# One more row's sums on ScalarE, one more front pair in plain form, and new hand-written orders

## The chip, the core and the metric

The program runs on one core of a Trainium2 chip. A core has a matrix engine (TensorE, PE in the profile; its weight loads are PEld), VectorE (DVE), ScalarE (ACT), GpSimd (POOL) and SyncE (SP), which here only issues DMAs. Each engine works through its own list of instructions in order and waits for the others by semaphores. Matmul results go to PSUM, which has eight banks of 512 float32 per partition; all else is kept in SBUF. The metric is the time of the program on the device in microseconds, lower is better. The kernel before takes 345.87 us, the median of three runs from 345.47 to 346.12.

## What is computed

Four residual blocks on one tensor of 2048 rows and 512 columns: a spectral filter A, a mixer B, then both again with the same weights. "Layer" below means one A and one B.

```python
def _A_ref(x, w_r, w_i):
    B, S, D = x.shape
    X = (lambda x, axes=(-2,-1): jnp.fft.rfft2(x.astype(jnp.float32), axes=axes))(x, axes=(-2, -1))
    W = w_r + 1j * w_i
    X = X * W
    y = (lambda x, s, axes=(-2,-1): jnp.fft.irfft2(x, s=s, axes=axes).astype(jnp.bfloat16))(X, (S, D), axes=(-2, -1))
    return y

def _B_ref(x, w1, w2, w3, w4):
    ...
    h = _gelu(_layernorm(x, axis=-1) @ w1)
    ...
    hs = jnp.concatenate([g0, g1, g2, g3], axis=-1) @ w2
    x1 = x + hs
    h2 = _gelu(_layernorm(x1, axis=-1) @ w3) @ w4
    return x1 + h2

x = A_x
x = x + _A_ref(_layernorm(x, axis=-1), A_w_r, A_w_i)
x = x + _B_ref(_layernorm(x, axis=-1), B_w1, B_w2, B_w3, B_w4)
x = x + _A_ref(_layernorm(x, axis=-1), A_w_r, A_w_i)
x = x + _B_ref(_layernorm(x, axis=-1), B_w1, B_w2, B_w3, B_w4)
```

`g0` to `g3` are quarters of the columns of `h`, shifted by one or two rows down or up. The FFTs are done as matmuls with tables of cosines and sines.

## The kernel before

Row s of x is held as s = 16 p + q: partition p, and one of 16 "rows" q of 128 x 512 elements. In the mixers row n of the order `ROWS` is q = n + 2 modulo 16. The kernel schedules nothing by itself: three strings, ORDER_0, ORDER_A and ORDER_B, list the steps, and each step appends its instructions to the engines concerned. So a step's place in the string is its place in the list of every engine that it uses. A step is a letter, a number, for some an engine (A ScalarE, V or D VectorE, P GpSimd), and after a point the PSUM bank.

- ORDER_0, the first front. `s` takes the sums of a row: by bn_stats on VectorE, or for rows in `ON_ACT` by two passes of ScalarE (lines 353 and 290), of which `f` makes mean and variance on GpSimd (lines 359 to 361). `i` aggregates (line 306), `S` is the square root on ScalarE, `J` the reciprocal on VectorE (line 368). These work by groups of rows, `GROUPS`. `Q` multiplies the DFT table by a row's 1/std into one of eight buffers Tq (lines 384, 386), `O` is the front's matmuls of a pair of rows (line 403), `G` and `L` copy the result to V (lines 152, 154; `L` is the second half of a split copy).
- ORDER_A and ORDER_B, layers 1 and 2. A: `d` (lines 544 to 550) and its copy `t`, `q` (line 568) and its copy `x`, the product with the filter `p` (line 587 from the copy; line 584 straight from PSUM when its engine is D), `b` and `V` (line 598) with copies `m` and `l`; then `D` and `C` (line 618), the copy `Y`, `P` (line 646), and `a` (line 654), which adds to x and takes the sums. B: `s` squares on ScalarE, `r`, `e`, `i`, `M`, `c` make 1/std, `n` normalises, `T` is the transposing DMA on SP (line 674), which is how rows turn into columns; `v` (line 686) multiplies by w1, `h` is gelu; `u` (line 702) multiplies by w2, `f` adds, `k` squares, `R`, `o`, `U` are the second norm and its transposing DMAs, `w` (line 737) multiplies by w3, `g` is gelu, `W` (line 757) multiplies by w4, `A` (line 763) adds to x. At the end of layer 2 `y` stores; at the end of layer 1 come the statistics `B`, `j`, `S`, `J` and the front of layer 2 (`Q`, `O`, `G`, `L`). `X` is so many matmuls on zeros.
- `over_p_quarters` and `over_p_plain` are two forms of the front. The quarters form folds inside the matmuls: a row takes four matmuls of 256 columns and four of 128, and ScalarE or VectorE copies to V. The plain form takes four matmuls of 128 columns a row; the right half is copied by ScalarE (`G..A`), two subtractions and an addition follow on VectorE (`G..V`, lines 424, 425), and `I` folds again (line 435). `PLAIN` says how many pairs of layer 2's front have it: pairs 0 to 5 of 0 to 6; rows 14 and 15 stand alone. A pair in `SPLIT_V` is copied in halves.

Transposing DMAs and stores share SP's list. V's buffer is that of xn. The copies t, X's junk rows, Y, `right` and `pairs` share four buffers of one tag (TV_Y).

Of the kernel before, what the change touches and what calls it, by code (L numbers as in the profile page):

```python
# [11 lines left out]
ACT = mybir.ActivationFunctionType  # L12
ALU = mybir.AluOpType
BF16 = dt.bfloat16
FP32 = dt.float32

P = 128
# [358 lines left out]
            self.K.nc.scalar.activation(dst, src, ACT.Identity, bias=self.mr[:, i, :], scale=r)  # L376

def scaled_T(K, q, r, eng="V"):

    K.Tq[q] = K.stream.tile([P, 2, P], BF16, name="Tq", bufs=8)
    if eng in "VP":
        e = K.nc.vector if eng == "V" else K.nc.gpsimd
        e.tensor_scalar(K.Tq[q][:], K.T[:], r, None, op0=ALU.mult)
    else:
        K.nc.scalar.activation(K.Tq[q][:], K.T[:], ACT.Copy, bias=0.0, scale=r)  # L386

def over_p_quarters(K, qs):

    n = len(qs)
    ps = banks(K, 2)
    for i, q in enumerate(qs):
        T = K.Tq.pop(q)
        plus, both, swap = [v.rearrange("d k (b c) -> d k b c", c=4) for v in (T[:], T[:], T[:, ::-1])]
        plus = plus[:, 0]
        twice = lambda k: T[:, k:k + 1].to_broadcast([P, 2, P]).rearrange("d k (b c) -> d k b c", c=4)
        for h in range(2):
            o = ps[:, h, 0:256 * n].rearrange("d (k b q c) -> d k b q c", k=2, q=n, c=4)[:, :, :, i]
            terms = ((0, o, twice(0)), (1, o[:, 1], plus), (3, o[:, 1], plus), (2, o, swap)) if h == 0 else \  # L400
                    ((1, o, swap), (0, o[:, 0], plus), (2, o[:, 0], plus), (3, o, twice(1)))
            for j, (c, dst, rhs) in enumerate(terms):
                K.nc.tensor.matmul(dst, lhsT=K.x[:, q, c * P:(c + 1) * P], rhs=rhs, start=(j == 0), stop=(j == 3))  # L403
    return ps[:, :, 0:256 * n]

def over_p_plain(K, qs):

    ps = banks(K, len(qs))
    for i, q in enumerate(qs):  # L410
# [41 lines left out]
def first_front(K):  # L452
# [71 lines left out]
def layer(K, last):  # L524
# [4 lines left out]
    V = K.V  # L529
# [6 lines left out]
    tv, X, pab, Y, xT, xT3, gT, ln, ln3, lnA = [{} for _ in range(10)]  # L536
# [251 lines left out]

    def scale_T(n, eng):
        k, i = divmod(n, 4) if n < 12 else (n, 0)  # L790
        scaled_T(K, ROWS[n], lnA[k].r[:, i:i + 1], eng)

    def front(k):
        qs = [ROWS[n] for n in PAIRS[k]]
        ps["O", k] = over_p_plain(K, qs) if k < PLAIN else over_p_quarters(K, qs)

    def take_front(k, eng, half=0):
        if "V" not in next_V:
            next_V["V"] = new_V(K)
        qs = [ROWS[n] for n in PAIRS[k]]  # L800
        if k < PLAIN:
            if eng == "A":
# [40 lines left out]
WAKE = 30  # L843
FILL = {}
GROUPS = [[0, 1], [2, 3], [4, 5, 6, 7], [8, 9, 10, 11], [12, 13], [14, 15]]
ON_ACT = [5, 9]
TABLES = 2
FIRST = [[0, 1], [2, 3], [4, 5], [6, 7], [8, 9], [10, 11], [12, 13], [14], [15]]
UNITS = {b: [b, b + 1] if 2 <= b < 14 else [b] for b in (0, 1, 2, 4, 6, 8, 10, 12, 14, 15)}
# [3 lines left out]
LATE = ((14, 15), (0, 14))  # L853
SPLIT_B = ((12, 13, 14, 15), (12, 13, 14, 15))
SPLIT_FIRST = (5, 6, 7, 8)
SPLIT_V = (6, 14, 15)
ROWS = [*range(2, 16), 0, 1]
PAIRS = {**{k: [2 * k, 2 * k + 1] for k in range(7)}, 14: [14], 15: [15]}
PLAIN = 6
FLEX = "mlGLnotxYIKEpQ"  # L860
FOLD = [(), ()]
ORDER_0 = """
s1 s0 i1 i0 S0 s2 s5 J0 Q0A Q1A s4 s7 s6 i4 f2 O0.4 i7 i6 S2 s3 J2 i2 s9 Q6V Q7V O3.0 i3 s11 S1 J1 s10 Q4A Q2A Q5A G3A
s8 i11 i10 i8 s12 f3 O2.2 Q3P O1.6 S3 J3 Q11P s13 i12 Q10A O5.0 s15 G0A i13 Q8A Q9P S4 G2A s14 i15 J4 Q12V i14 O4.4 S5
J5 Q15V G1A G5V Q13P O6.2 L5A O8.0 Q14V O7.6 G4A G6V G7A L7A G8V L6V L8V
"""
ORDER_A = """
d2.2 t2V d0.6 t0A d1.0 d4.4 N0 q0.6 t1A q2.2 d6.0 x0V p0V q1.6 t4A q4.4 x2A d10.2 t6A d8.0 p1D b1.6 p2P t10A b0.7
q10.2 p4D m0V t8A q6.0 d14.4 m1A d12.6 x10A t14V p10V x6A d15.2 t12A p6V b2.5 b4.3 m4A q14.0 q12.6 x14A q8.3 p12D b3.0
m2A b10.1 b11.5 x8A b7.4 t15A p14P q15.2 b5.6 b14.7 m10A b6.1 m11A b12.5 m7A m5A m3A b13.4 m6A p8V b8.6 m12A p15D b9.0  # L870
m8A b15.2 m15A V12.1 m13V V13.3 l12A m14V V15.4 V14.5 m9V l15V D3.0 l14V D1.6 l13A C1 C3 D0.2 C0 Y1A P3.4 P2.5 Y0A Y3V
a3 s3 P6.0 a2 s2 P1.1 P0.6 a1 a0 s1 P7.2 D2.4 C2 D5.6 s0 a7 s7 D7.2 C5 Y2V P5.1 r0 e0 i0 a6 Y5A a5 D4.4 s6 s5 P4.0 M0
n3V a4 n0V n2P s4 n1P D6.6 C7 C6 Y6A P11.0 T1 C4 P10.1 Y7V P15.2 r1 e1 a11 P12.3 i1 M1 n7V T0 Y4A n6V s11 n5A T3 P13.6
P9.5 n4V a10 s10 P8.4 a8 s8 v1.0 a9 s9 P14.7 a13 s13 h1 v0.4 a14 T2 c0 h0 r2 n8P v3.6 h3 v2.0 h2 n9V T4 a15 c1 n10V
n11V u0.5 a12 u3.4 u1.0 f3 u2.1 s12 f2 s14 s15 r3 n14V T5 v5.2 n15V v4.6 c3 T7 k3 h5 u4.1 n12V h4 u7.4 n13V f0 k0 T6
u6.5 f1 k1 u5.6 c2 E3V f7 E7V E2V f4 k2 R0 o2V f6 o3A v6.2 h6 v7.0 h7 f5 E1P E6V o1P k4 E0V o0V u12.4 k6 k7 k5 R1 U1
o7A u9.5 u15.3 f9 U0 u13.1 f12 E12V u10.7 k12 E4P u14.0 u11.5 o6P U3 E5V o5A f15 u8.2 w0.3 k15 E9P g0 f8 k8 o4P f11
E11V k11 w4.5 g4 w3.2 f14 k14 f10 w2.4 E10P g3 E8P w5.2 w1.6 g2 E14V g5 U2 w7.2 g1 f13 k13 R3 w6.0 k9 k10 w8.5 g6 W3.7
A3 B3 g8 W2.0 R2 A2 B2 o9P o10A W1.5 W0.0 g7 A1 B1 o11A U5 o8A j1 E15V U4 w14.2 g14 w11.4 w12.2 g11 w9.4 w10.6 g9 j2
w13.4 E13P g12 g10 g13 W7.1 o13V W5.2 A0 w17.4 W4.0 j3 B0 w16.6 j0 S0 Q2V Q3V A7 A4 Q1P B7 o12P W6.3 A5 A6 B6 g16 j7  # L880
w15.0 g15 w19.2 g19 B4 w18.0 g18 g17 w20.6 j4 j6 g20 o14A B5 W11.0 j5 S1 U6 Q6V W9.1 Q4P o15P U7 A11 B11 w21.6 Q5A
O2.2 O1.4 Q7A G1A j11 A9 B9 W8.0 G2A G2V Q0P O0.2 G1V A8 I1V I2V B8 j8 g21 w24.6 W10.1 A10 B10 j10 G0A g24 w23.6 j9 S2
Q11P Q9P g23 w22.0 O3.4 w26.6 g22 w27.0 G3A G3V G0V g26 Q8P I3V w25.4 g27 I0V g25 W13.2 A13 B13 j13 O4.0 G4A G4V I4V
W12.3 A12 B12 j12 S12 S13 J13 Q13P J12 W15.1 A15 B15 j15 S15 J15 Q15A W14.2 W24.5 Q12A Q10V O5.6 A14 A24 O6.2 G5A B14
B24 j14 S14 G6A J14 Q14A L6A O15.0 G15A L15A O14.2 G14A G5V I5V L14A
"""
# [17 lines left out]

# [28 lines left out]
```

## Time and profile before

| what | value |
|---|---|
| median of three runs | 345.87 us |
| the profiled execution | 346.01 us, of which its span 344.2 us |
| TensorE clock granted | 1.000 of full over the span |
| PE, ACT, DVE, POOL busy | 335.5, 195.6, 165.0, 107.1 us |
| first matmul of the front | at 7.73 us |
| layer 1: first `d`, first `D`, first `v`, first `w` | 19.4, 37.1, 51.8, 80.1 us |
| layer 2: first `d`, first `D`, first `v`, first `w` | 183.6, 202.0, 216.5, 244.5 us |

The span runs from the first to the last instruction in the profile; the rest of the execution, 1.8 us, lies around it. PE counts as busy from the start of a matmul to its modelled end, so 97% busy hides small losses between matmuls; the starts of the matmuls show them.

### The profile page before, as it was taken

Reading aid. Unit: us, or ns where it says so; the run is one execution under the profiler, and the core shown is the slowest. Engines: PE = TensorE matmul, PEld = TensorE weight load, DVE = VectorE, ACT = ScalarE, POOL = GpSimd, SP = SyncE. Lnnn points to the kernel's source line nnn. Section 1 sums busy time; section 2 is a strip of 40 time slices with the busy share of each in tenths; the row PEclk is TensorE's granted clock in tenths of the full one; section 3 lists DMA queues with packets and bytes.
Section 4 is the critical chain, followed back from the end, with each engine's and each line's share of the span. In section 5 each row is a group of like instructions: output and inputs, shape, how many; then the busy total and the mean of one; then the engine's idle time right before and its main releaser. Section 6 shows DMA issues by size and latency. Waiting matters only on the chain.

```text
span 344.2 us, 5699 instructions
## 1 busy us (share of the span) xinstructions
PE 335.5 (97%) x2171; PEld 187.6 (55%) x2189; DVE 165.0 (48%) x377; ACT 195.6 (57%) x357; POOL 107.1 (31%) x200
## 2 busy tenths in 40 slices
PE   7999999999999999999999999999999999999996
PEld 5878974444444444454467888444444444444443
DVE  4889895685035015264676979647802000110122
ACT  4979899768752403534538979968681446014300
POOL 2884066668242000304011404765591000000000
PEclk9999999999999999999999999999999999999999
DMA  7986986333030100300000002541403500000121
GB/s 257 314 295 230 372 202 113 72 61 62 3 61 0 32 0 0 31 2 0 2 0 2 2 3 47 104 81 20 89 0 76 109 0 0 30 18 5 41 78 46
DMA packets 45259, 24.60 MB, mean 71 GB/s; under 512 B 35072, under 2 KB 42240, under 8 KB 45232
## 3 DMA queue, kind: packets, MB, share of 16 engines
q1 hardware_dynamic: 43760, 19.74, 23.5%
q0 software_dynamic: 1232, 4.40, 3.7%
q8 instruction: 17, 0.28, 0.3%
q10 hardware_dynamic: 240, 0.10, 0.1%
q14 instruction: 10, 0.08, 0.1%
HBM read 11.61 MB, written 2.10 MB: 40 GB/s over the span
## 4 chain that ended last, share of the span: by engine, by line
PE 87%; DMA 4%; DVE 4%; ACT 2%; issue 1%; SPq 0%; POOL 0%; ACTq 0%; DVEq 0%; POOLq 0%
PE ps L737 28%; PE ps L757 26%; PE ps L686 8%; PE ps L702 8%; PE ps L598 4%; PE ps L403 3%; PE ps L618 3%; PE ps L568 2%; DMA xT<-xn 2%; PE ps L550 2%; PE ps L646 2%; DMA x_state<-in_A_x_dram 1%; DVE x_state L654 1%; ACT xn L290 1%; ACT gT L744 1%
## 5 line engine op out<-in xcount | busy, mean ns | idle before, releaser
L744 ACT ACTIVATE gT<-ps 128x1024 bf16<-128x1024 f32 x56 | 55.8, 1022 | 86.1 <-PE ps L737 86.1
L737 PE MATMUL ps<-xT,w 128*128 128x512 bf16 x448 | 99.2, 379 | 0.5 <-DMA xT<-xn 0.5
L757 PE MATMUL ps<-w,gT 128*128 128x512 bf16 (+2 forms) x462 | 97.8, 366 | 0.7
L763 DVE TENSOR_TENSOR x_state<-ps,x_state 128x512 bf16<-128x512 f32 (+2 forms) x34 | 22.2, 659 | 124.5 <-PE ps L757 124.5
L757 PEld LDWEIGHTS <-gT 128*128 128x128 bf16 x476 | 45.5, 98 | 51.4
L737 PEld LDWEIGHTS <-w 128*128 128x128 bf16 x448 | 43.7, 98 | 53.1 <-DMA xT<-xn 1.0
L710 DVE SCALAR_TENSOR_TENSOR xn<-xn,ln_c,ps 128x512 bf16<-128x512 bf16 x32 | 23.0, 743 | 15.5 <-PE ps L702 8.8
L686 PE MATMUL ps<-xT,w 128*128 128x512 bf16 x128 | 28.9, 379 | 0.7 <-DMA xT<-xn 0.4
L702 PE MATMUL ps<-w,hT 128*128 128x512 bf16 x124 | 28.3, 379 | 0.2
L290 ACT ACTIVATE junk<-xn 128x512 bf16<-128x512 bf16 x32 | 19.7, 622 | 4.8 <-DVE xn L710 4.8
L278 DVE BATCH_NORM_STATS2 ln_st<-x_state 128x6 f32<-128x512 bf16 (+2 forms) x31 | 20.2, 663 | 3.9 <-DMA x_state<-in_A_x_dram 3.6
L654 DVE SCALAR_TENSOR_TENSOR x_state<-ps,x_state 128x512 bf16<-128x512 f32 x32 | 20.7, 684 | 1.3 <-PE ps L646 1.2
L686 PEld LDWEIGHTS <-w 128*128 128x128 bf16 x128 | 12.3, 98 | 15.9 <-issue 1.7
L702 PEld LDWEIGHTS <-hT 128*128 128x128 bf16 x128 | 12.4, 98 | 15.3 <-ACT hT L693 0.4
L290 ACT ACTIVATE xn<-x_state 128x512 bf16<-128x512 bf16 x32 | 19.8, 620 | 0.9 <-DVE x_state L654 0.7
L693 ACT ACTIVATE hT<-ps 128x512 bf16<-128x512 f32 x32 | 17.4, 601 | 4.6 <-PE ps L686 4.4
L313 POOL TENSOR_SCALAR ln_ve<-ln_mv 128x4 f32<-128x4 f32 x11 | 2.8, 257 | 54.6 <-DVE ln_mv L306 53.9
L646 PE MATMUL ps<-Y,Tinv 128*128 128x256 bf16 x128 | 16.0, 272 | 0.1
L598 PE MATMUL ps<-TR,PB 128*128 128x128 bf16 x256 | 16.0, 219 | 0.0
L584 DVE TENSOR_TENSOR PB<-ps,W 128x1024 bf16<-128x1024 f32 x13 | 15.4, 1217 | 0.7 <-PE ps L568 0.5
L618 PE MATMUL ps<-G,hT 128*128 128x256 bf16 x128 | 15.7, 272 | 0.0
L403 PE MATMUL ps<-Tq,x_state 128*128 128x256 bf16 (+1 forms) x160 | 14.0, 246 | 1.6 <-ACT Tq L386 1.0
(95 smaller groups left out, 405.9 us busy)
## 6 DMA issues: line engine op xcount, KB each, us to landing
w<-in_B_w_dram SPq DMA_DIRECT2D x2, 1792.0 KB, 14.3
W<-W POOLq DMA_DIRECT2D x4, 514.0 KB, 5.0
x_state<-in_A_x_dram SPq DMA_DIRECT2D x8, 256.0 KB, 4.7
out_dram<-x_state SPq DMA_DIRECT2D x15, 128.0 KB, 1.9
w<-in_B_w_dram SPq DMA_DIRECT2D x2, 512.0 KB, 6.2
W<-in_A_w_r_dram SPq DMA_DIRECT2D x7, 128.5 KB, 5.8
W<-in_A_w_i_dram SPq DMA_DIRECT2D x7, 128.5 KB, 5.9
TL<-tab_TL POOLq DMA_DIRECT2D x3, 256.0 KB, 5.4
```

The lines of the kernel that those rows point to most:

```text
L290: K.nc.scalar.activation(out, src, ACT.Square, bias=0.0, scale=D ** -0.5, accum_out=self.s[:, i, 1:2])
L403: K.nc.tensor.matmul(dst, lhsT=K.x[:, q, c * P:(c + 1) * P], rhs=rhs, start=(j == 0), stop=(j == 3))
L598: nc.tensor.matmul(o[:, k0 * P:(k0 + 1) * P], lhsT=pab[u][:, k, 2 * (b - u) + h, f * P:(f + 1) * P], rhs=K.TR[:, k:k + 2, 2 * b + h], star ...
L618: nc.tensor.matmul(o[:, i, e * 256:(e + 1) * 256], lhsT=M[:, F, e, 2 * m + i, :], rhs=K.G[:, F, e, :], start=(F == 0 and e == 0), stop=(F ...
L646: nc.tensor.matmul(o[:, h * 256:(h + 1) * 256], lhsT=K.Tinv[:, c], rhs=rhs[:, ::-1] if h else rhs, start=(e == 0), stop=(e == 1))
L654: nc.vector.scalar_tensor_tensor(K.x[:, q, :], ps.pop(("P", q)), 1.0, K.x[:, q, :], op0=ALU.mult, op1=ALU.add, accum_out=ln[g].s[:, i, 0:1])
L686: nc.tensor.matmul(o[:, i], lhsT=K.w1[:, t, j * P:(j + 1) * P], rhs=xT[g][:, :, t, :], start=(t == 0), stop=(t == 3))
L702: nc.tensor.matmul(o, lhsT=K.hT[:, j, st:st + P], rhs=K.w2[:, j, :], start=(j == 0), stop=(j == 3))
L710: nc.vector.scalar_tensor_tensor(xn[:, q, :], xn[:, q, :], ln[q // 4].c[:, q % 4:q % 4 + 1], ps.pop(("u", n)), op0=ALU.mult, op1=ALU.add, ...
L737: nc.tensor.matmul(o[:, i], lhsT=K.w3[:, c, t * P:(t + 1) * P], rhs=xT3[g][:, :, c, :], start=(c == 0), stop=(c == 3))
L744: nc.scalar.activation(gT[g][:, 2 * j:2 * j + 2, :], ps.pop(("w", k)), ACT.Gelu_apprx_tanh, bias=0.0, scale=1.0)
L757: nc.tensor.matmul(o, lhsT=gT[g][:, t, i * P:(i + 1) * P], rhs=K.w4[:, t, d], start=(t == 0), stop=(t == 13))
```

## The change

A third row, 1, has its sums taken on ScalarE in the first front. Pair 6 of layer 2's front (rows 12 and 13 of `ROWS`) goes from the quarters form, copied in two halves, to the plain form with the folds on VectorE (`G6V`, `I6V`). Tables for pairs in plain form are scaled in one sign only, 128 columns in place of 256. All three orders are written anew: engines, places and PSUM banks of many steps differ. The number of steps of each kind is the same but for `f0` in place of `i1`, for pair 6, for the filter's products (ORDER_A has no `x0`, `x10` and has `x15`; ORDER_B has no `x4` and has `x1`, `x15`) and for the matmuls on zeros (`X9` new in layer 1, `X6` for `X3` in layer 2). The diff, cut to the stretches that the prediction speaks of:

```diff
-def scaled_T(K, q, r, eng="V"):
-
-    K.Tq[q] = K.stream.tile([P, 2, P], BF16, name="Tq", bufs=8)
+def scaled_T(K, q, r, eng="V", signs=2):
+
+    K.Tq[q] = K.stream.tile([P, signs, P], BF16, name="Tq", bufs=8, padded_shape=[P, 2, P])
     if eng in "VP":
         e = K.nc.vector if eng == "V" else K.nc.gpsimd
-        e.tensor_scalar(K.Tq[q][:], K.T[:], r, None, op0=ALU.mult)
+        e.tensor_scalar(K.Tq[q][:], K.T[:, 0:signs], r, None, op0=ALU.mult)
     else:
-        K.nc.scalar.activation(K.Tq[q][:], K.T[:], ACT.Copy, bias=0.0, scale=r)
+        K.nc.scalar.activation(K.Tq[q][:], K.T[:, 0:signs], ACT.Copy, bias=0.0, scale=r)
...
-        scaled_T(K, ROWS[n], lnA[k].r[:, i:i + 1], eng)
+        scaled_T(K, ROWS[n], lnA[k].r[:, i:i + 1], eng, 1 if n < 2 * PLAIN else 2)
...
-ON_ACT = [5, 9]
+ON_ACT = [1, 5, 9]
...
-SPLIT_V = (6, 14, 15)
+SPLIT_V = (14, 15)
...
-PLAIN = 6
+PLAIN = 7
...
 ORDER_0 = """
-s1 s0 i1 i0 S0 s2 s5 J0 Q0A Q1A s4 s7 s6 i4 f2 O0.4 i7 i6 S2 s3 J2 i2 s9 Q6V Q7V O3.0 i3 s11 S1 J1 s10 Q4A Q2A Q5A G3A
-s8 i11 i10 i8 s12 f3 O2.2 Q3P O1.6 S3 J3 Q11P s13 i12 Q10A O5.0 s15 G0A i13 Q8A Q9P S4 G2A s14 i15 J4 Q12V i14 O4.4 S5
-J5 Q15V G1A G5V Q13P O6.2 L5A O8.0 Q14V O7.6 G4A G6V G7A L7A G8V L6V L8V
+s1 f0 s5 f2 s0 s3 i3 s2 i0 s4 S0 i2 J0 S1 s6 Q0A Q1A J1 Q3A Q2A O0.2 s7 i4 i6 i7 s10 O1.4 S2 J2 s9 f3 s11 Q4V Q6V Q5A
+s8 G0A i11 i10 i8 S3 J3 Q7A s12 s13 O2.6 s15 s14 i13 O3.0 Q10A Q11A O5.2 i12 i14 G1A G2A Q8P S4 i15 J4 Q12V S5 J5 Q14V
+Q15V Q9P O4.4 Q13A O6.6 G3V G4A G5A L6V O8.4 L5A G6A O7.0 L8A G8V G7V L7A
 """
 ORDER_A = """
...
-a3 s3 P6.0 a2 s2 P1.1 P0.6 a1 a0 s1 P7.2 D2.4 C2 D5.6 s0 a7 s7 D7.2 C5 Y2V P5.1 r0 e0 i0 a6 Y5A a5 D4.4 s6 s5 P4.0 M0
-n3V a4 n0V n2P s4 n1P D6.6 C7 C6 Y6A P11.0 T1 C4 P10.1 Y7V P15.2 r1 e1 a11 P12.3 i1 M1 n7V T0 Y4A n6V s11 n5A T3 P13.6
-P9.5 n4V a10 s10 P8.4 a8 s8 v1.0 a9 s9 P14.7 a13 s13 h1 v0.4 a14 T2 c0 h0 r2 n8P v3.6 h3 v2.0 h2 n9V T4 a15 c1 n10V
-n11V u0.5 a12 u3.4 u1.0 f3 u2.1 s12 f2 s14 s15 r3 n14V T5 v5.2 n15V v4.6 c3 T7 k3 h5 u4.1 n12V h4 u7.4 n13V f0 k0 T6
...
+P7.1 a3 P0.3 P1.0 a2 s3 a0 s2 a1 P6.2 s0 D2.6 s1 a6 s6 C2 D5.4 Y2V r0 D4.2 e0 i0 M0 a7 C5 P4.0 a4 n1P P5.6 a5 Y5A
+P10.7 n0P s7 C4 D7.0 C7 s4 T0 D6.5 a10 s5 n2V n3V P11.4 C6 Y7A P15.7 T1 Y4V P8.0 r1 e1 s10 i1 M1 n7A n6P T3 n4A P14.1
+Y6V a11 s11 P9.2 a8 P12.3 P13.6 s8 a9 s9 a13 n5P T2 v1.4 h1 a12 a15 r2 s12 n10P n8P s15 v0.2 h0 v3.6 c1 v2.4 h3 u0.0
+n11V h2 a14 s14 s13 r3 n13P n9V u2.4 f2 k2 T5 n14V T4 u3.1 v5.3 v4.6 u1.2 n12V n15A h5 u4.3 h4 u5.4 u6.6 u7.5 f3 c0 f0
...
-w15.0 g15 w19.2 g19 B4 w18.0 g18 g17 w20.6 j4 j6 g20 o14A B5 W11.0 j5 S1 U6 Q6V W9.1 Q4P o15P U7 A11 B11 w21.6 Q5A
...
-W12.3 A12 B12 j12 S12 S13 J13 Q13P J12 W15.1 A15 B15 j15 S15 J15 Q15A W14.2 W24.5 Q12A Q10V O5.6 A14 A24 O6.2 G5A B14
-B24 j14 S14 G6A J14 Q14A L6A O15.0 G15A L15A O14.2 G14A G5V I5V L14A
...
+g10 A0 w12.4 B2 B0 j1 j2 g12 g13 j0 E8P o8V U4 j3 S0 Q2V W4.0 W5.1 Q3A O1.2 A4 B4 j4 G1A w14.4 U7 G1V W7.0 W6.6 g14 A7
...
+O5.6 B12 I4P j12 S12 A13 B13 j13 G5A G5V I5P W15.5 A15 S13 J13 Q13A J12 B15 j15 W14.7 A14 S15 W24.5 J15 Q15A A24 B14
+B24 j14 Q12P O6.6 G6A S14 J14 O15.2 G15A Q14A X9.4 O14.0 G14A L14A G6V I6V L15A
 """
 ORDER_B = """
-X3.4 d4.1 d15.0 t15V d12.5 d1.7 t4A q4.0 t1V t12A q15.2 d0.4 d2.6 p15D x4A q1.0 d8.2 t0A q0.4 t2A t8A q2.6 p1D x0A
...
-n0A P10.5 a10 s10 P15.0 T1 n1P T0 P9.1 a9 s11 c1 s9 r2 v2.2 a13 a15 v3.5 a14 n9P n8V T4 h2 v1.0 s15 h3 h1 v0.2 u3.4 h0
...
+X6.4 d4.4 d1.7 t1V d12.2 d15.0 t15V t4A q4.4 q1.6 t12A x1A q15.1 d0.0 d2.6 p1P x15A d8.2 t0A t2A q0.0 p4D t8V q12.4
...
+D7.4 a1 P12.2 C7 s1 D5.0 M1 n5P n4P n6V T2 C5 Y7A P13.3 n7V T3 Y4V P8.5 r0 e0 i0 P9.4 Y5A M0 n2A n3P T1 P11.1 a12 a8
+n0P s12 a9 a11 s9 s8 P14.6 P10.0 a10 P15.7 s10 a14 s11 v3.1 n1P T0 v2.4 a15 s15 a13 v0.6 h3 r2 n9V n10V h2 h0 n11V T5
+c0 n8V v1.1 h1 u2.5 s14 u3.4 s13 c1 r3 f3 T4 n13A n14P E3V u0.6 f0 u1.7 n15V k3 v5.0 n12V h5 v4.2 u4.4 h4 T6 f2 k2
...
```

## The prediction

> **What bounds the kernel now.** I read the page's busy times first, then its chain, then who PE waited for.
>
> ```profile
> span 344.2 us, 5699 instructions
> ...
> PE 335.5 (97%) x2171; PEld 187.6 (55%) x2189; DVE 165.0 (48%) x377; ACT 195.6 (57%) x357; POOL 107.1 (31%) x200
> ...
> PE 87%; DMA 4%; DVE 4%; ACT 2%; issue 1%; SPq 0%; POOL 0%; ACTq 0%; DVEq 0%; POOLq 0%
> ```
>
> Matmuls bound it. The chain shows 80 matmuls of 512 columns in 17.27 us, 0.216 each; a matmul of n columns is priced at 0.216 x n/512 below. So a change of orders can gain only what PE now waits, and lose without a limit. The waits (total, times, longest):
>
> ```profile
> PE ps L403 <- ACT Tq L386: 1.0, 2, 0.8
> ...
> PE ps L403 <- DVE Tq L384: 0.6, 1, 0.6
> PE ps L568 <- DVE PB L584: 0.5, 1, 0.5
> PE ps L737 <- DMA xT<-xn: 0.5, 1, 0.5
> PE ps L686 <- DMA xT<-xn: 0.4, 1, 0.4
> ```
>
> They lie in the first front, the spectral stages, the turn into the mixer, one transposing DMA late in layer 1, and the step from layer 1 to 2; the two MLPs have almost none. I follow the new order through these places, each engine's list in turn, with the durations of the rows. Nothing else is assumed to move.
>
> **1. First front: +0.35 us (-0.2 to +0.8).** x's DMAs land at 4.20 (rows 0, 1), 4.87, 5.90, 7.22. Before, VectorE does both rows, S0 runs at 5.76, row 5's sums stand between S0 and Q0A, and the first matmul is at 7.73. Now ScalarE does row 1 (4.22 to 5.45; one row is 1.23 from mean to next free) and, ahead of S0, row 5 (5.92 to 7.15, when its DMA is there). S0 at 7.15, J0 behind i2 at 7.6, Q0A 7.8 to 8.3, first matmul 8.34: 0.6 late. But rows 2 and 3 follow at once (S1 stands beside S0): the second pair starts at 9.65, before at 9.78, so the wait of 0.6 us is gone. Later pairs: Q4V at 10.97 (0.05 late), Q7A behind G0A and S3 (0.1), and Q12V behind four bn_stats (4 x 0.65), i and J4, at 16.6 when PE comes at 16.25 (0.4). Then ScalarE has six copies (0.9, 4 of 0.5, 0.35 and 0.35 back to back, one of them freed by DVE) and ends at about 20.0; the first `d` needs them; its second matmul stood at 19.77. Sum of the walk +0.25; I take +0.35, as the six copies have no slack.
>
> **2. Spectral stages: layer 1 0 (+-0.5), layer 2 -0.3 (-0.9 to +0.6).** Busy time in first `d` to first `D` of each layer (columns: length, PE, PEld, DVE, ACT, POOL):
>
> ```profile
> 19.77:37.06 17.29, 17.29 (x256) 14.67 (x257) 15.97 (x19) 16.02 (x27) 9.34 (x8) 1.00 0.75 256
> 183.91:202.00 18.09, 17.56 (x255) 14.54 (x256) 15.86 (x17) 16.80 (x26) 5.50 (x2) 1.00 0.01 2
> ```
>
> ScalarE and VectorE are both over 88% busy: the copies out of PSUM bound these stages as much as PE. Layer 1: x10 gone (-1.05 ACT), x15 and t14 new on ACT (+0.63, +0.62), one full m less (-0.66), a half m more (+0.48): 0.0; VectorE loses x0 and t14 (-0.69 each), p0 and p10 now read PSUM (+0.53, +1.05), p15 the copy (-0.53), m's +0.26: -0.1. Nothing. Layer 2: t8 goes to VectorE (-1.03 ACT, +1.22 DVE), x4 goes (-1.05), x1 and x15 come (+1.26): ACT -0.8. VectorE: t8 +1.22, p1 and p15 to GpSimd -2.44, p4 to VectorE +2.43, p6 to GpSimd -1.38: -0.2. Together 1.0 less over two engines, 0.5 each; I take 0.3.
>
> A rule speaks against this. The Trainium skill, "SBUF — State Buffer", section "SBUF: two separate sides", says that GpSimd and a VectorE instruction with two SBUF inputs take a shared port pair as an exclusive lock, so the second blocks fully. GpSimd gets 3.8 us more of products here (two of 1.92; p6 at 3.75 for p4). The row: the same VectorE form with and without GpSimd beside it.
>
> ```profile
> 192.13 2.20 DVE L587 TENSOR_TENSOR PB<-X,W 128x2048 bf16<-128x2048 bf16 x1
> ...
> 194.85 1.21 DVE L587 TENSOR_TENSOR PB<-X,W 128x2048 bf16<-128x2048 bf16 x1
> ```
>
> By the row a meeting costs 1.0 us on VectorE, by the rule up to GpSimd's whole 3.75. The new order puts p12V and p8V behind p0P and ahead of p6P, whose neighbour p10 reads PSUM; so I count no meeting, and keep +0.6 in the range.
>
> **3. From P to v in layer 1: +0.25 (-0.3 to +0.6).** The chain to the first transposing DMAs is unchanged: sums of a0 to a3 end where they did, M0 at 45.05, two norms of 0.8 on GpSimd, T0 at 46.9, T1 at 48.3, landing at 51.63 as now. The order puts all 16 P ahead of v, so 0.43 us of work (P14) moves into the wait of 0.56 before v1. It comes back later: T2 waits for n5P behind n6P (T2 lands 55.5, PE is at v3 by 55.2: 0.25), and ScalarE now does squares s12 and s15 (2 x 0.62) between h1 and h0, where before seven halves of gelu ran without a break from 55.46. h3 ends at 59.2 and h2 at 60.3, when u0 and u2 stand ready at 59.0 and 60.1: 0.25 and 0.2. -0.43 + 0.25 + 0.45 = +0.27.
>
> **4. The late transposing DMA in layer 1: -0.65 (-0.67 to 0).**
>
> ```profile
> 142.42 4.57 DMA xT<-xn
> 147.03 1.90 PE ps L737 x8
> ```
>
> U6 waits for o14A and PE for U6; start to start 0.67 us too much. In the new order o14 and o15 are on GpSimd many steps earlier, and U4 to U7 precede their first w by at least 4 us of w and W (from w7's end: four squares, R2, o's and U's end at +13, w14 comes at +17.7). The wait goes; behind it nothing is late.
>
> **5. Step from layer 1 to layer 2: +0.55 (0 to +1.0).**
>
> ```profile
> 179.73 0.29 DVE x_state L763
> 180.02 0.67 DVE ln_st L278 x2
> 180.72 0.22 DVE ln_mv L306
> ...
> 181.28 0.60 ACT V L154
> 181.88 0.40 ACT Tq L386
> ...
> 182.32 0.98 PE ps L403 x8
> 183.30 0.33 PE ps L262 x3
> ```
>
> Row 14's chain (A24, B, j, S, J, Q14) decides, not PE: W24 ends at 179.6 and O14 can't start before 182.3. Before, PE fills that with O5, O6 and O15 (0.43 + 1.30 + 0.65). Pair 6 in plain form saves 16 matmuls of 3,072 columns and adds 8 of 1,024: -0.86 us of PE. But that work stood inside this wait, so nothing is saved; the 9 new matmuls on zeros (9 x 0.108 = 0.97) sit in the hole. And O5 moves ahead of W24, out of the hole: +0.43. On the chain itself, G15A (0.37) stands ahead of Q14A instead of a copy of 0.60: -0.2. After O14, three half copies on ScalarE (G14, L14, L15) replace two: +0.35, and X6's 0.65 us lies beside them. VectorE's G6V and I6V (0.74 + 0.68 + 0.76) run from J14 at 181.5 to 183.7 beside O14 and the copies. 0.43 - 0.2 + 0.35 = +0.58. The 128-column tables (not in the trace: ScalarE between the 0.29 of a 4-column row and 0.50, VectorE 0.16 to 0.29, GpSimd 0.25 to 0.94) are early enough to count as nothing.
>
> On the zeros, the Trainium skill, "TensorE: Matmul & The Clock Gate", section "Part 1: The HAM clock gate", says that PE's clock halves only after an idle window of about 3.4 us. The granted clock here is 1.000 with PE holes of 0.4 us; by the rule a hole of 1 us without the zeros would leave it so. I give X9 neither gain nor cost, and 0.97 us of cost if the hole closes.
>
> **6. From P to v in layer 2: +0.45 (0 to +0.9).** Y4V now stands behind n6V and n7V on VectorE and ends at 213.9, P8 waits 0.65 for it, but the bank of v3 waits for a11 to 216.75 anyway (before 216.47), and T0 lands at 220.1 as now: +0.1. Then six squares stand ahead of the table load (218.35 before, 219.4 now), gelu h1 of the last v starts at 224.0, and u2, the first u, needs it; before the first u was u3. +0.35.
>
> **7. The rest: +0.3 (0 to +1.0).** Over 200 us of two MLPs PE has almost no wait, with 56 gelus, 34 additions and 32 transposing DMAs just in time. New orders can only add here. The last steps (W20, A10, A20, y20) stand on their engines as before.
>
> **Sum:** 0.35 + 0 - 0.3 + 0.25 - 0.65 + 0.55 + 0.45 + 0.3 = +0.95. On the profiled execution's 346.01 us that is 346.96; it lies 0.14 over the median of the runs, 345.87, so the median after should be about **346.8 us**.
>
> **Rivals.** (a) *Faster: ScalarE's load in the spectral stages decides.* If all of the 0.8 us that ScalarE loses in layer 2 shows on PE, layer 1 gains 0.3 from better places, and parts 6 and 7 cost only 0.1 and 0, the sum is 0.35 - 0.3 - 0.8 + 0.25 - 0.65 + 0.55 + 0.1 = -0.5; without the front's late copies -0.9: **345.0**. It decides from about 0.6 us gained in layer 2's stage. For it: 16.8 of 18.1 us busy. Against: VectorE stays as full. Chance 0.26. (b) *No change: gains and losses cancel*, parts 6 and 7 cost little: **346.0**. For it: every part is under 0.7 us. Chance 0.27. (c) *GpSimd's longer list blocks*: n, o and p on GpSimd meet VectorE in several places at 1 us each, or make a transposing DMA late; two such meetings on top of the sum give **348.8**. Chance 0.12. (d) *Pair 6 saves what it saves on paper*: -0.86 in part 5 instead of +0.55 would give 345.4; the chain of row 14 speaks against it; it is counted in (a) and (b). The forecast itself, +0.3 to +2 us: 0.35.
>
> 0.2% is 0.69 us, about what a measurement of this kernel can tell from no change. Faster by more 0.26, within 0.27, slower 0.47. The range runs from 344.7 to 348.8; the forecast's own from 346.2 to 347.9.
>
> **What would show it.** First matmul of the front at 8.3 and the second pair before 9.8; first `D` of layer 2 at most 18.1 us behind its first `d`; no PE wait on line 737; 4.3 to 4.5 us from W24's end to the first `d` of layer 2; a wait of the first u in both layers. Wrong if the spectral stages move by over 0.7 us, or if an MLP shows waits of PE on ScalarE or on a DMA.

## The result, and the profile after

The changed kernel takes **344.94 us** (median of 20 runs, 344.23 to 346.22) against 346.04 us for the kernel before beside it: ratio 0.9972, 95% interval 0.9963 to 0.9981, some 0.97 us less. The forecast was 346.8 us and slower. The time lies inside the range, but the direction was wrong. It is rival (a)'s time, 345.0, and in part by luck: layer 2's spectral stage did gain what (a) says, but (a) also has layer 1's spectral stage gain 0.3 us and the late transposing DMA 0.65. The first lost 0.59, and the second was worth some 0.4.

From the page of the profiled execution (345.21 us, span 343.3), the lines that answer to those of before:

```profile
span 343.3 us, 5708 instructions
...
PE 335.5 (98%) x2174; PEld 188.5 (55%) x2193; DVE 162.5 (47%) x373; ACT 193.6 (56%) x359; POOL 115.1 (34%) x213
...
PE 76%; ACT 9%; DMA 6%; POOL 3%; DVE 3%; issue 1%; SPq 1%; ACTq 0%; POOLq 0%; DVEq 0%
```

PE is busy for the same 335.5 us in a span 0.9 us shorter. So what was gained is waits, as the prediction held; the question is which. Whom PE waited for (total, times, longest):

```profile
PE ps L262 <- DVE zeros L253: 1.0, 1, 1.0
PE ps L403 <- ACT Tq L386: 1.0, 1, 1.0
PE ps L544 <- DVE V L152: 0.3, 1, 0.3
PE ps L686 <- DMA xT<-xn: 0.2, 1, 0.2
```

Gone are the second wait of the front (line 384, 0.6), the one on a product (line 568, 0.5) and the late transposing DMA (line 737, 0.5). Of the waits that the prediction put in their place, those on gelu and on `T2` are not here. A wait on the front's last copies is (line 544, 0.28), but before had it too, as two waits of 0.14 and 0.17.

One profile isn't enough to read differences of some tenths: the changed kernel was profiled twice, and its spans were 343.3 and 344.2 us. So the table takes each stage from several profiles of this study: those of kernels that have before's order there, and those that have the changed one. A profile whose experiment touches that very stage is left out of its row (`e_p14` of the third, `e_o14` of the fourth, `e_quart` of the fifth, `e_lock`, `e_t8` and `e_layer2` of the sixth). The second row takes only profiles in which the front and the order are both before's or both changed; the mixed ones come at the end of the experiments. "Predicted" is the prediction's own sum, with `O5`'s 0.43 us counted where it stands, ahead of `W24`.

| stage (start to start, on PE) | order of before: mean (range, profiles) | changed order: mean (range, profiles) | measured | predicted |
|---|---|---|---|---|
| start to second matmul of `d`, layer 1 | 19.87 (19.62-20.31, 7) | 19.47 (19.33-19.65, 9) | -0.40 | +0.35 |
| to `D`, layer 1 | 17.29 (17.29-17.30, 6) | 17.88 (17.40-18.55, 6) | +0.59 | 0 |
| to first `u`, layer 1 | 22.22 (21.87-22.94, 6) | 21.67 (21.37-22.41, 9) | -0.55 | +0.25 |
| to last `W24` | 120.06 (119.62-120.48, 6) | 120.08 (120.07-120.11, 9) | 0.0 | -0.22 |
| to second matmul of `d`, layer 2 | 4.44 (4.43-4.44, 7) | 4.21 (4.20-4.21, 8) | -0.23 | +0.12 |
| to `D`, layer 2 | 18.09 (18.09-18.10, 6) | 17.35 (17.34-17.36, 7) | -0.74 | -0.3 |
| to first `u`, layer 2 | 21.78 (21.45-21.91, 7) | 21.76 (21.54-21.89, 9) | 0.0 | +0.45 |
| to the last matmul | 117.40 (117.39-117.44, 7) | 117.61 (117.54-117.76, 9) | +0.2 | +0.3 |
| sum | | | -1.1 | +0.95 |

The step into layer 2 and its spectral stage (the fifth and sixth) repeat to 0.02 us. Those in which a DMA is awaited (the first, the third, and the fourth in before's order) vary by 0.3 to 1.1 us from profile to profile with the same code; the second varies only in the changed order. `e_layer2` reaches its second `d` late, so it is counted from the first: 17.67 us to `D`, against 18.36 before and 17.60 in the changed kernel. So nearly all of the gain in the sixth row belongs to that order.

### The profile page after: what moved, and what is told of

It is laid out like the page before. It is cut to its first block, busy times and chain, and to the rows that moved or that the text cites. A ratio compares the mean times of both kernels' runs of the same rounds, so it can differ in the third digit from the quotient of the medians.

```text
span 343.3 us, 5708 instructions
## 1 busy us (share of the span) xinstructions
PE 335.5 (98%) x2174; PEld 188.5 (55%) x2193; DVE 162.5 (47%) x373; ACT 193.6 (56%) x359; POOL 115.1 (34%) x213
## 4 chain that ended last, share of the span: by engine, by line
PE 76%; ACT 9%; DMA 6%; POOL 3%; DVE 3%; issue 1%; SPq 1%; ACTq 0%; POOLq 0%; DVEq 0%
PE ps L737 28%; PE ps L757 28%; PE ps L702 6%; PE ps L598 4%; PE ps L686 4%; DMA W<-in_A_w_i_dram 4%; ACT xn L290 3%; ACT hT L693 2%; PE ps L568 1%; PE ps L618 1%; DMA W<-in_A_w_r_dram 1%; POOL PB L587 1%; DVE x_state L654 1%; PE ps L550 1%; DMA xT<-xn 1%
## 5 line engine op out<-in xcount | busy, mean ns | idle before, releaser
L278 DVE BATCH_NORM_STATS2 ln_st<-x_state 128x6 f32<-128x512 bf16 (+2 forms) x30 | 19.4, 662 | 4.0 <-DMA x_state<-in_A_x_dram 3.7
L587 POOL TENSOR_TENSOR PB<-X,W 128x1024 bf16<-128x1024 bf16 (+1 forms) x6 | 15.9, 2661 | 13.2 <-ACT X L154 13.2
L584 DVE TENSOR_TENSOR PB<-ps,W 128x1024 bf16<-128x1024 f32 x15 | 17.5, 1214 | 0.1
L296 POOL TENSOR_SCALAR ln_mv<-ln_s 128x4 f32<-128x4 f32 x16 | 4.3, 268 | 33.5 <-DVE x_state L654 20.1
```

What stands on the lines that cost most here:

```text
L278: self.K.nc.vector.bn_stats(self.st[i][:, int(k)], src)
```

## The experiments

Each time is a median in us, "before" the kernel before, measured beside it on the same chip.

### The three parts alone

`e_front` is the kernel before with the changed front, `e_layer1` with the changed order of layer 1, `e_layer2` with that of layer 2.

```
e_front:  ORDER_0 of the changed kernel; ON_ACT = [1, 5, 9]
e_layer1: ORDER_A of the changed kernel; PLAIN = 7, SPLIT_V = (14, 15), sign columns
e_layer2: ORDER_B of the changed kernel
```

> The kernel before with the new first front alone (ORDER_0, row 1 on ScalarE). Theory 1, the gain is the sum of what the stage starts of the two profiles differ by, stage by stage: first matmul of the front 0.62 us later, second matmul of the first d of layer 1 0.14 us earlier, and the kernel 0.1 to 0.2 us faster. Rival (the recorded sum): the late copies of ScalarE show, first d 0.25 us later and the kernel 0.35 us slower.

> The kernel before with the new order of layer 1 alone (ORDER_A, pair 6 plain, tables of one sign). Theory 1: +0.4 us in the spectral stage, -0.3 from D to u, -0.7 at the late transposing DMA, +0.2 at the step to layer 2, in sum 0.4 us faster. Rival (the recorded sum, parts 2 to 5): +0.15 us. A second rival, that the stages lean on the front that stands before them: then the spectral stage's +0.4 does not appear here.

> The kernel before with the new order of layer 2 alone (ORDER_B). Theory 1: first d to first D 0.75 us shorter than the 18.09 us of before, the rest of the layer 0.25 us longer, the kernel 0.5 us faster. Rival (the recorded sum, parts 2, 6, 7): -0.3 + 0.45 + 0.15 = +0.3 us slower.

| | this | before | ratio (95%) |
|---|---|---|---|
| `e_front` | 345.29 | 346.11 | 0.9987 (0.9968 to 1.0005) |
| `e_layer1` | 345.24 | 346.11 | 0.9977 (0.9968 to 0.9987) |
| `e_layer2` | 345.63 | 346.11 | 0.9991 (0.9977 to 1.0005) |

Layer 1's order alone is faster; for the other two the intervals hold 1, and the stages tell more. (The three gains add up to more than the whole one, 0.45% against 0.28%; their intervals are wide enough for that.) The front: second matmul of `d` at 19.52, before's fronts at 19.87 on average. The changed kernel's front, as the timeline shows it (start, busy time, engine, line, instruction, count):

```profile
8.35 10.79 PE L403 MATMUL ps<-Tq,x_state 128*128 128x256 bf16 x128 [0.98 <-ACT Tq L386]
...
12.53 2.44 DVE L278 BATCH_NORM_STATS2 ln_st<-x_state 128x6 f32<-128x512 bf16 x4
...
16.47 3.10 ACT L154 ACTIVATE V<-ps 128x1024 bf16<-128x1024 f32 x6
```

The first matmul stands at 8.35, as predicted, and from there PE has one unbroken group of 128. Of the waits for `Q4V`, `Q7A` and `Q12V` (0.05 + 0.1 + 0.4) at most 0.08 us is left: the pairs start 1.32 us apart, the one that needs `Q12V` 1.40. Four bn_stats take 2.44 us, 0.61 each, where the walk had 0.65. `J4`'s reciprocal stands at 15.63, and `Q12V` is done at 16.2 in place of 16.6. The six copies end at 19.57 in place of 20.0.

Over all profiles the front's gain is made at the second pair. It starts at 9.51 us on average with the new front (9.34 to 9.69, nine profiles) and at 9.90 with before's (9.67 to 10.32, seven); from there to the second `d` both take the same, 9.96 and 9.97 us. The first matmul is only 0.2 us later on average (8.19 against 7.98); the 7.73 of before's profile was one of its early ones.

From `P` to `u` in layer 1, the changed kernel's ScalarE and PE:

```profile
52.19 7.07 PE L686 MATMUL ps<-xT,w 128*128 128x512 bf16 x32 [0.23 <-DMA xT<-xn]
...
53.24 1.28 ACT L693 ACT_TABLE_LOAD   x1
54.53 1.08 ACT L693 ACTIVATE hT<-ps 128x512 bf16<-128x512 f32 x2
...
56.73 3.17 ACT L693 ACTIVATE hT<-ps 128x512 bf16<-128x512 f32 x6
...
59.10 2.10 PE L702 MATMUL ps<-w,hT 128*128 128x512 bf16 x8
```

The two squares do stand between the gelus of `h1` and `h0`, as predicted. But the table load is there at 53.24, 0.9 earlier than before, and six gelu halves take 3.17 us, a start every 0.51. `u0` has its data, and all 32 matmuls of `v` run in one piece, so `T2` is in time too.

### P14 ahead of v, alone

```
-... P8.4 a8 s8 v1.0 a9 s9 P14.7 a13 ...
+... P8.4 P14.7 a8 s8 v1.0 a9 s9 a13 ...
```

> The kernel before with one step moved: the last P of layer 1 (P14) ahead of the first v, where PE waits 0.56 us for a transposing DMA, in place of behind it. Theory 1, P14 fills the wait and what follows has slack: the first u stands 0.4 us earlier (58.7 in place of 59.1 us) or, if the gelus that u needs are the limit, at the same time. The recorded sum says that the waits come back: +0.45 of 0.43 us. So: -0.4 us by the theory, 0 by the recorded step.

345.7 against 346.06, ratio 0.9987 (0.9974 to 0.9999). First `v` to first `u` of layer 1 is 6.97 us; it is 7.34 in all six profiles of before's order, where `P14` stands between the `v`. PE's list in this run:

```profile
48.83 3.04 PE L646 MATMUL ps<-Y,Tinv 128*128 128x256 bf16 x25
51.70 7.12 PE L686 MATMUL ps<-xT,w 128*128 128x512 bf16 x32
58.67 1.67 PE L702 MATMUL ps<-w,hT 128*128 128x512 bf16 x7
```

All 32 `v` in one piece and `u` right behind. So work moved into a wait stays gained here. This run has neither `n5P` behind `n6P` nor the squares between the gelus, from which the prediction let 0.25 + 0.45 come back; for these the changed order itself speaks. In all nine profiles that have it, first `v` to first `u` takes 6.90 to 6.91 us: 0.43 less than before, the work of `P14`, and nothing has come back. From `D` to the first `v`, where `P14` now stands, the changed order takes no longer (14.46 to 15.51 us, before 14.53 to 15.60).

### The late transposing DMA, alone

```
-... w19.2 g19 B4 w18.0 g18 g17 w20.6 j4 j6 g20 o14A B5 ...
+... w19.2 g19 B4 o14A w18.0 g18 g17 w20.6 j4 j6 g20 B5 ...
```

> The kernel before with one step moved: the norm o14 on ScalarE ahead of the gelus of w17, w18 and w20 in place of behind them, so that its transposing DMA U7 starts about 2 us earlier. Theory 1: the wait of 0.67 us at 146 us goes, nothing else is late, the kernel is 0.6 to 0.7 us faster. Rival: the gelus pushed back by 0.8 us make w or W wait for banks, and no more than 0.3 us is won.

345.8 against 346.06, ratio 0.9989 (0.9979 to 1.0). The wait on line 737 is gone and the stage takes 119.69 us. In six runs that left this order alone it took 120.06 on average, but in two kinds: 120.37, 120.29 and 120.48 where the DMA of `U7` took 4.57, 4.49 and 4.67 us to land, and 119.62, 119.75 and 119.85 where it took 3.56, 3.95 and 4.05. (The prediction wrote `U6`; the one that waits for `o14` and `o15` is `U7`.) So the wait of before's profile comes in half of the profiles, and taking it away is worth 0.37 us on average, not 0.67. The changed kernel's stage says the same: 120.08, less the 0.43 of `O5` that came into it, is 119.65.

### The meeting of GpSimd and VectorE in layer 2

```
-... p8V b8.0 p0P b9.2 ...
+... p8V b8.0 p0V b9.2 ...
```

> The kernel before with one step of layer 2 changed: the product p0 on VectorE in place of GpSimd. VectorE gets 0.65 us more work, but its p12, which took 2.20 us beside GpSimd's p0, should take 1.2. Theory 2, the meeting of the two engines at p12 is what made PE wait 0.69 us in the spectral stage of layer 2: that wait shrinks to under 0.3 us and the kernel is 0.2 to 0.6 us faster. Rival, VectorE's sum of work decides and not the meeting: VectorE has 0.65 us more, the stage is 0.3 to 0.6 us longer.

345.85 against 346.11, ratio 0.9989 (0.9979 to 0.9999). The timeline of VectorE in this run, at the place where the instruction of 2.20 us stood before:

```profile
191.18 1.22 DVE L587 TENSOR_TENSOR PB<-X,W 128x2048 bf16<-128x2048 bf16 x1
192.31 0.69 DVE L152 CAST hT<-ps 128x512 bf16<-128x512 f32 x1
192.91 1.82 DVE L587 TENSOR_TENSOR PB<-X,W 128x2048 bf16<-128x2048 bf16 x2
```

With nothing beside it on GpSimd the product takes 1.22 us. VectorE does one product more, and still the stage is 17.72 instead of 18.09: ending the meeting is worth **0.37 us** on PE. PE's wait on VectorE's product there, 0.53 us before, is 0.25. (`p0` itself is also shorter on VectorE, 0.69 us in place of 1.92; what that alone is worth was not tried.)

What the meeting costs VectorE can be read from GpSimd's line of before:

```profile
187.74 5.50 POOL L587 TENSOR_TENSOR PB<-X,W 128x2048 bf16<-128x2048 bf16 x2 [10.54 <-ACT X L154]
```

It ends at 193.24, 1.11 us after VectorE's product began (192.13), and that product took 0.99 us longer than alone. In other profiles what was left of GpSimd's product and what VectorE's took longer are 0.65 and 0.54 us (`e_front`, at 28.39), 0.40 and 0.27 (the changed kernel, at 192.42), 0.18 and 0.06 (`e_wbefore`, at 28.71). So a meeting has no fixed price: VectorE's product, where it starts second, loses the rest of GpSimd's, less 0.1 us. This agrees with the rule that the prediction set against its row; the 1.0 us was the rest of a product of 1.92.

In the changed order only a short rest is met: VectorE's `p12` and `p8`, between two groups of GpSimd's,

```profile
186.96 5.86 POOL L587 TENSOR_TENSOR PB<-X,W 128x1024 bf16<-128x1024 bf16 x3 [8.96 <-ACT X L154]
...
192.42 2.62 DVE L587 TENSOR_TENSOR PB<-X,W 128x2048 bf16<-128x2048 bf16 x2
...
194.85 3.92 POOL L587 TENSOR_TENSOR PB<-X,W 128x2048 bf16<-128x2048 bf16 x1 [2.04 <-ACT X L154]
```

take 2.62 for two; GpSimd's first group ends at 192.82, so only the first of them is touched, by 0.27.

### ScalarE's load in layer 2: t8 back on it

```
-... x15A d8.2 t0A t2A q0.0 p4D t8V q12.4
+... x15A d8.2 t0A t2A q0.0 p4D t8A q12.4
```

> The changed kernel with one copy of layer 2's spectral stage back on ScalarE (t8: +1.03 us there, -1.22 on VectorE). Theory 3, ScalarE's load decides the stage: first d to first D grows by 0.5 to 1.0 us from 17.34. Rival, VectorE's load decides: it shrinks by 0.3 or more. If neither (the chain of waits of single steps decides): within 0.25 us.

345.5 against 345.92, ratio 0.9991 (0.9984 to 0.9998). `d` to `D` of layer 2 is 17.91 us, in the changed kernel 17.35. With this copy of 1.03 us on ScalarE the stage is **0.56 us** longer, and PE's list shows where:

```profile
189.71 0.22 PE L544 MATMUL ps<-FL,V 128*128 128x128 bf16 x1 [0.66 <-ACT X L154]
```

It is one wait, behind a copy of ScalarE's. So the copy's place in the list may matter as much as the sum of ScalarE's work; this run can't tell them apart. Nor can its 0.56 be added to the 0.37 of the meeting: it is the price in the changed order, and in before's order PE had no wait on ScalarE here but 0.04 at the start; the other was 0.53 on VectorE. Of the 0.74 us that the stage gained, `e_lock` shows 0.37. The rest goes with the lighter lists of ScalarE and VectorE, and which of its moves made it stays open.

### The step from layer 1 to layer 2: zeros and quarters

`e_nozeros` is the changed kernel without the nine matmuls on zeros; `e_quart` also puts row pair 6 back into its form of before.

```
e_nozeros: -... Q14A X9.4 O14.0 ...              +... Q14A O14.0 ...
e_quart:   -... X9.4 O14.0 G14A L14A G6V I6V L15A   +... O14.0 G14A L14A L6V L15A
           -PLAIN = 7, SPLIT_V = (14, 15)        +PLAIN = 6, SPLIT_V = (6, 14, 15)
```

> The changed kernel without the nine matmuls on zeros ahead of the last front pair of layer 1. If the hole that they sit in is PE's wait for row 14's table, the step from layer 1 to 2 is as long as with them and the kernel the same within 0.2 us. If the clock falls in a hole of 1 us, the granted clock drops under 1.00 there and the next matmuls take twice as long: +0.3 us or more. If they delay PE (the table was there at 181.75, the pair starts at 181.81), 0.1 us faster.

> The changed kernel with pair 6 of layer 2's front back in the quarters form, copied in two halves, and without the nine matmuls on zeros; the order is else the new one. The plain form's saving of 0.86 us of PE lies in PE's wait for row 14's table: then the time is the same within 0.2 us. If the saving reaches the end, this is 0.5 to 0.9 us slower. If VectorE's folds cost more than they save, this is faster by 0.1 to 0.3.

| | this | before | ratio (95%) | step |
|---|---|---|---|---|
| `e_nozeros` | 344.61 | 346.06 | 0.9950 (0.9934 to 0.9966) | 4.21 |
| `e_quart` | 345.12 | 346.06 | 0.9970 (0.9961 to 0.9979) | 4.45 |

PE's list of `e_nozeros`, and below it a window over its step (length, then busy time and count of PE, PEld, DVE, ACT, POOL; then PE's clock):

```profile
181.18 0.82 PE L403 MATMUL ps<-Tq,x_state 128*128 128x256 bf16 x8 [1.12 <-ACT Tq L386]
```

```profile
179.10:184.00 4.90, 3.71 (x40) 2.98 (x38) 3.13 (x10) 3.13 (x9) 0.00 (x0) 1.00 0.00 0
```

A hole of 1.12 us, the clock stays at 1.00, the step is as long as with zeros: the nine matmuls neither help nor cost, as predicted. Pair 6 in plain form is worth 0.24 us here, neither the 0.86 of its matmuls nor nothing. All of it lies ahead of `O14`, which starts 2.88 us after the last `W24` in `e_quart`: there ScalarE's copy of pair 6 waits for the longer `O6` and begins at 181.03, and `S14`, behind it in ScalarE's list and with its data at 181.24, begins at 181.52. The changed kernel's step itself:

```profile
181.25 0.50 ACT L386 ACTIVATE Tq<-T,ln_r 128x256 bf16<-128x256 bf16 x1
...
181.81 0.82 PE L403 MATMUL ps<-Tq,x_state 128*128 128x256 bf16 x8
...
182.33 0.99 ACT L154 ACTIVATE V<-ps 128x256 bf16<-128x256 f32 x3 [0.58 <-PE ps L403]
```

`O14` starts at 181.81, 2.64 after the last `W24` at 179.17; before 2.85 (182.32 - 179.47). These 0.2 us are what the prediction expected of the shorter `G15A` ahead of `Q14A`; but `e_quart` has `G15A` there too and gains nothing, so it takes pair 6's plain form as well. After `O14`, three half copies end 0.99 after they begin, 0.33 apiece, and they begin 0.52 after `O14`. PE's second `d` is at 183.38, 1.57 after `O14`.

### Layer 1's spectral stage: order or filter loads

The changed kernel's front ends 0.4 earlier, and the `D` of layer 1 begins no earlier than before. In the changed kernel the chain of waits runs through the filter's loads (start, length):

```profile
17.98 4.92 DMA W<-in_A_w_i_dram
...
24.96 3.88 POOL PB L587
28.84 0.05 issue
28.89 0.62 PE ps L598 x8
```

In the kernel before it runs through PE alone. So there are two readings: products wait for the filter, or the new order's copies are too late. `e_spec1` has before's order of this stage in the changed kernel, `e_best` also leaves out the zeros; `e_wafter` and `e_wbefore` load one filter chunk once more, ahead of the 16; `e_after` is the changed kernel again.

```
e_spec1:  ORDER_A up to l15V as before, then D3.0 l14V D1.6 l13A C1 C3 ...
e_best:   the same, and -X9.4
e_wafter, e_wbefore, ahead of the filter's chunks:
+    nc.sync.dma_start(extra.rearrange("p (j f) -> p j f", f=257), planes[0][:, 0:8])
```

> The changed kernel with the spectral stage of layer 1 in the order before, up to the first D. Theory 1, the stage's +0.41 us (17.71 from the second matmul of the first d to the first D, 17.29 before) belongs to that order: the stage takes 17.3 us again and the kernel is 0.3 to 0.4 us faster than the changed one. Rival, it belongs to what the new front leaves behind (GpSimd's and the queues' state, loads in flight): the stage stays at 17.6 or more, no gain.

> The changed kernel once more, as the neighbour of the next three. Both theories: about 344.9 us, first matmul of the front near 8.35, first D of layer 1 near 37.2 (36.9 to 37.6) whatever the front did, step from W24's end to layer 2's first d 4.21 us, layer 2 from d to D 17.35 us.

> The changed kernel with one chunk of the filter loaded once more ahead of the 16 chunks, into memory that is overwritten later. These loads land 0.36 to 1.6 us apart, 0.77 on average, so all later ones land some 0.7 us later. Theory (in layer 1 the front's gain is given back because products wait for the filter's loads): the first d stays, the first D of layer 1 moves 0.4 to 0.8 later, the time is 0.4 to 0.8 us longer than the changed kernel's. Rival (copies on ScalarE and VectorE set that stage): D within 0.2 of where it was, the time too.

> The kernel before with the same extra chunk. Theory: PE itself carries the chain of layer 1's spectral stage here and the filter has some 0.25 us to spare (first D at 37.06; with the new front and the old order at 36.80), so D moves 0 to 0.5 us, less than in the changed kernel. Rival (the filter has no part in it): nothing moves.

> The changed kernel with layer 1's spectral stage in the order of the kernel before, and without the nine matmuls on zeros. Theory: the order of before is 0.2 us shorter there (D at 36.8), the zeros are worth 0: about 344.5 us, 0.3 to 0.5 less than the changed kernel. Rival (the lower time of that order alone was chance between calls): 344.9, as the changed kernel.

| | this | before | ratio (95%) | `d` to `D` | last filter chunk lands |
|---|---|---|---|---|---|
| `e_spec1` | 344.56 | 345.92 | 0.9957 (0.9945 to 0.9970) | 17.47 | 22.64 |
| `e_after` | 344.80 | 345.89 | 0.9961 (0.9947 to 0.9976) | 18.22 | 22.26 |
| `e_wafter` | 344.42 | 345.89 | 0.9961 (0.9948 to 0.9974) | 17.68 | 22.97 |
| `e_wbefore` | 345.68 | 345.89 | 1.0003 (0.9989 to 1.0017) | 17.30 | 23.04 |
| `e_best` | 344.30 | 345.89 | 0.9953 (0.9937 to 0.9968) | 17.39 | 22.77 |

The extra chunk missed its aim in the changed kernel: the last chunk landed at 22.97, where it landed at 22.89 and 22.26 without. It can't be said that anything was delayed, and nothing moved. In the kernel before, the last chunk landed at 23.04 instead of 21.98, and the stage kept its 17.30: with that order and that front the filter has 1 us to spare. `e_best` tells more. Windows over the stage of the changed kernel, then of `e_best`:

```profile
19.62:37.33 17.71, 17.31 (x256) 14.60 (x256) 16.05 (x18) 16.22 (x27) 8.71 (x7) 1.00 0.87 304
```

```profile
19.53:36.92 17.39, 17.36 (x257) 14.61 (x256) 16.02 (x19) 16.05 (x27) 8.41 (x7) 1.00 0.86 287
```

The same front and nearly the same load on every engine; in the changed order PE is idle for 0.40 us, in before's order for 0.03. The 0.40 are three waits, which end at 22.83, 26.81 and 28.89 us: 0.13 for a copy `TV` of ScalarE, 0.12 for a product of VectorE, 0.15 for GpSimd's first product. Only the last hangs on the filter, so a chain through `W<-in_A_w_i_dram` for 4% of the span, on the page, stood for 0.15 us of PE's time in this stage: a chain names the last to arrive, by however little. In `e_after` there was another:

```profile
PE ps L598 <- DMA TR<-tab_TR: 0.6, 1, 0.6
```

The first two waits are in all six profiles of the changed kernel's front and order, and in none with before's order. So the order costs some 0.25 us on a copy and a product, and loads take the rest, differing from run to run (17.40 to 18.55).

How late the filter may be shows when the profiles are set side by side, by the time from the second `d` to the landing of the last chunk. In before's order the stage is 17.29 us where this time is up to 3.19 (`e_wbefore`), then 17.39 at 3.24 (`e_best`), 17.47 at 3.31 (`e_spec1`) and 17.73 at 3.58 (`e_front`). In the changed order it is 17.40 at 2.62 (`e_t8`), 17.68 to 17.72 at 3.27 to 3.32 (three profiles) and 18.55 at 4.12 (`e_quart`). So the filter counts from about 3.2 us on, and a front that ends 0.4 us earlier brings every profile that much nearer to it. No run delayed the loads alone, and one profile doesn't fit: `e_layer1`, with before's front, takes 17.96 at 3.32, with waits of 0.36 and 0.29 on products of VectorE. So the new order loses behind the old front too, and why it loses more there is open.

`e_best` has the lowest median of all, and the order of before in this stage is the better one by the stage's length; as times, its interval overlaps that of `e_after`, so a gain over the changed kernel isn't proved.

## Why the prediction was wrong

1. **First front: wrong in sign.** First matmul at 8.35 (predicted 8.34), second pair at 9.67 (9.65). The waits from `Q4V` on (0.55 in the walk) and the late copies did not come, and the wait that went stayed gained: -0.40 against +0.35. The walk's own terms don't give its +0.25 either: -0.13 at the second pair and +0.55 make +0.42. And the gain at the second pair was taken from one profile as 0.13; on average it is 0.39.
2. **Spectral stages: two terms mis-sized, in opposite directions.** Layer 2 gave -0.74, not -0.3. A meeting had been read as 1.0 us of VectorE's time, but the one that *goes* was not counted as a gain; it is worth 0.37 alone. ScalarE's load was halved by argument; one copy of 1.03 us put back costs 0.56, though at one place of the changed order. Rival (a)'s deciding point, 0.6, was passed, and so was the prediction's own sign of being wrong, 0.7. Layer 1 gave +0.59 instead of 0. Counting sums of copies can't show that a copy and a product come 0.13 and 0.12 us late, and the filter's loads were in no list that was walked.
3. **P to v in layer 1: the step that failed most clearly.** "It comes back later": 0.25 for `T2` and 0.45 for gelu. Nothing came back: from first `v` to first `u` PE takes 6.90 to 6.91 us in nine profiles, 7.34 before. The -0.43 for `P14` was right, and the +0.70 behind it was wrong. The squares stand where the walk had them, but ScalarE came to its table load 0.9 us sooner than before, and T2's rows landed at 55.18 (52.06 + 3.12) where PE came to `v3` at 55.6. The other 0.1 us of the -0.55 lies ahead of the first `v` and is within the scatter there.
4. **The late DMA: mechanism right, size wrong.** The wait on line 737 is gone. Its 0.65 us was read from one landing of 4.57 us; the mean of several runs is about 0.4, which `O5`'s 0.43 in the same stage uses up.
5. **The step to layer 2: direction wrong by 0.35.** The row chain does decide, the matmuls saved don't count in full, and the zeros are free. The term that failed is "three half copies on ScalarE (G14, L14, L15) replace two: +0.35": from `O14`'s start to the second `d` it was 1.57 us after and 1.59 before (183.91 - 182.32). "Nothing is saved" by pair 6 was wrong as well, by 0.24 us, through ScalarE's list and not through PE's; rival (d)'s 0.86 fell with it.
6. **P to v in layer 2: +0.45 predicted, 0 measured.** The squares do stand ahead of the table load. That starts 16.97 us after `D` (217.69 - 200.72), where the walk has 17.4 (219.4 - 202.0), and the eight gelu halves need 4.08 us, so that the last pair starts some 21.3 us after `D` and not 22.0:

```profile
217.69 1.28 ACT L693 ACT_TABLE_LOAD   x1
218.99 4.08 ACT L693 ACTIVATE hT<-ps 128x512 bf16<-128x512 f32 x8
```

`u` starts at 222.49, without a wait.

7. **The rest: right**, +0.2 for +0.3, in layer 2's MLP.

Parts 1, 3 and 6, three walks through waits that would appear, make 2.0 of the 2.05 us between forecast and measurement (0.75, 0.80, 0.45); the other errors cancel. Each wait predicted there was 0.05 to 0.4 us, no larger than the error of the walk where it can be read (0.4 us at `Q12V`, 0.9 at layer 1's table load, 0.7 at layer 2's last gelu pair). Where the walk came out late, the lateness was counted in full; where it came out early, as nothing. So errors of the walk, in whichever direction, could only add to the sum.

Of the signs named beforehand, the front's two starts, the 18.1 us and the wait on line 737 came as said. The step into layer 2 did not (4.3 to 4.5 us from W24's end to the first `d`; it got 0.2 us shorter), nor did a wait of the first `u` in either layer.

## What to carry to other kernels

A predicted wait that is shorter than the error of the walk to it is no forecast: put it at half with both signs open, and keep removed waits that PE is seen to spend as the firmer term. But read a removed wait from several executions if a DMA ends it. And when a stage's engines are all nearly full, look first for the instruction that is longer than its neighbours of the same form, and ask what ran beside it: here such a one, made short again, gave 0.37 us.

## What was not expected of the hardware

- Instructions in a row on ScalarE and VectorE start closer than their own recorded time: eight gelu halves in 4.08 us (0.50 from start to start, (4.08 - 0.60)/7) where the page has 0.602 for one; four bn_stats in 2.44 (0.59 from start to start) where one of that shape has 0.680 on average. A walk that adds up mean durations is late by 0.05 to 0.1 us each.
- A VectorE product with both inputs in SBUF that starts while GpSimd runs such a product ends late by what is left of GpSimd's, less 0.1 us: 0.99 for 1.11, 0.54 for 0.65, 0.27 for 0.40.
- One and the same transposing DMA took 3.56 to 4.67 us from issue to landing in six profiles in which nothing around it was changed.
